# Transposes by VectorE instead of TensorE, transfers in other steps, and later phases in source order, in a fused state-space and two-layer feed-forward kernel

## The chip, the cores and the metric

The kernel runs on one core of one Trainium2 chip. The time is the device time of one execution in microseconds; several executions are measured and the median is told. A profile of one more execution gives the trace, whose times are counted from its first instruction. Engines are called by the profile's names: PE (TensorE), PEld (its weight loads), ACT (ScalarE), DVE (VectorE), POOL (GpSimd), SP (SyncE, which issues all DMAs here).

## The reference

Three stages, one behind the other, all in float32 at the interface:

```python
# 1. state-space attention: batch 4, 8 heads, 768 positions, head size 32, state size 16
cum = cumsum(log(clip(a)))                        # within a chunk
y   = ((C @ B.T) * exp(cum_i - cum_j) * causal) @ x  +  (C @ state) * exp(cum_i)
state = exp(sum) * state + sum_j B_j x_j exp(cum_last - cum_j)
# 2. x: (3072, 256), the heads side by side
h = max(x @ w1, x @ w2, x @ w3)                   # (3072, 768)
y = h @ w_out                                     # (3072, 256)
# 3.
h = y @ w_in                                      # (3072, 2048)
out = (max(h, 0) + alpha * min(h, 0)) @ w_out2    # (3072, 256)
```

The weights come as float64. The result is the same for any chunk length in stage 1.

## The kernel before

**Feed-forward layers.** Every operand is kept as two halves, a rounded one and the rest, and a product is three matmuls (`parts`, L582). Tokens go in six tiles of 512. Layer 1 has six units per tile (128 of 768 inner features): `up1` does three times six matmuls, ACT and DVE take the maximum, `halves` splits the result on ACT (`gh`) and POOL (`gl`). Layer 2 has sixteen units per tile: `up2` does six matmuls, two DVE instructions, then `halves`. `down` does six matmuls for a unit and comes two units after its `up` (`LAG`). The order of tiles is in `PHASES`: (1,0), (1,1), (2,0), (1,2), (2,1), (1,3), (2,2), (1,4), (2,3), (1,5), (2,4), (2,5), layer first; the fourth phase is (1,2). The two last `down`s of a phase are carried into the next one's first two units. They end with `end1` (L644), which splits a layer-1 tile into `yt`, or with `end2` (L652), which copies the transposed result out of PSUM (ACT one half, DVE the other), transposes it back with eight PE transposes in two batches (L664), copies each batch out and stores it. Both phases' accumulators are the same two PSUM banks.

**Attention.** 24 blocks of 128 positions of one sequence with all heads. Blocks 0 to 11 (two sequences) are direct: chunks of 64, nothing passes through DRAM. Blocks 12 to 23 are wide (`r >= NDIR`): one chunk of 128. For a wide block `att_t` (L337) transposes B, C and the decayed C (`cp`, none in the first block of a sequence) on PE (L344), copies them out and splits B and C in halves on ACT and DVE (L347 to L355), and stores the halves in a DRAM tile `sc` (L357). `att_l` loads them back in eight DMAs in a layout in which four heads stack on the partitions (L374, L376). `att_b` multiplies C with B (L419) and with the decay (L421). `att_e` makes the decay: eight exponentials on ACT (L402), two masks on POOL (L403). `att_a` multiplies B and C by their decays on POOL (L335), `att_y` makes the result (L487, L490) and its halves `xt` (L520, L521), `att_u` the state, and asks for the next rows of the cumulative sums (L321).

**Order.** The first blocks, up to L737, are written out in order by hand, in a manual schedule. Behind that a planner orders each engine's instructions by itself, from priorities and estimated times; the source gives it the work in this order: between the units, `attend` takes the next steps of a list (`rounds`, L524), so many that the blocks are done a little ahead of the tile that needs them (`quota`), and `slot` takes steps of the weights' conversion. A round has five steps. PE, ACT, DVE, POOL and SP each execute their instructions in the order that came out.

Of the kernel before, what the change touches and what calls it, by code (L numbers as in the profile page):

```python
# [9 lines left out]
F32 = mybir.dt.float32  # L10
# [9 lines left out]
P = 128  # L20
# [17 lines left out]

LEADW = 12288
START = 4  # L40
LAG = 2
# [33 lines left out]
def fused(ctx: ExitStack, tc: tile.TileContext, x, a, B, C, w1, w2, w3, w_out, v_in, v_out, alpha, cst, out):  # L75
# [133 lines left out]
    def load(r):  # L209
        if r < NR:  # L210
            load_bc(r)
            load_x(r)

    def load_bc(r):
        b, k = divmod(r, NB)
# [6 lines left out]
    def load_x(r):  # L222
        b, k = divmod(r, NB)
        d = blk[r]
# [11 lines left out]
    s_cum = yy.tile([P, 2, 512], F32R, tag="yt0", name="yt0").rearrange("p a b -> p (a b)")[:BT * H, :S].bitcast(F32)  # L236
    s_la = const.tile([P, NB, BT * H], F32, name="la")
    first = const.tile([P, Q], F32, name="first")
    never = const.tile([P, Q], BF16, name="never")
    one_b = const.tile([P, P], BF16, name="one_b")  # L240
    warm = un.tile([P, 512], F32, tag="g", name="g")[:, :256].bitcast(BF16)
# [86 lines left out]
    def att_a(r, only=None):  # L328
        b, k = divmod(r, NB)
        d = blk[r]  # L330
        for key, src, w, used in (("bp", "b", dec_b, r < NDIR or k < NB - 1), ("cp", "c", dec_c, r < NDIR or k)):
# [3 lines left out]
            nc.gpsimd.tensor_tensor(o, d[src], w[:, k, b, :].unsqueeze(2).to_broadcast([P, H, N]), ALU.mult)  # L335

    def att_t(r, part=None):  # L337
        d = blk[r]
        keys = [("b", "c"), ("cp",), ("b", "c", "cp")][2 if part is None else part]
        if r >= NDIR and r % NB == 0:  # L340
            keys = ("b", "c")
        pt = ptile(ps_at, "at", (P, 3, P)) if part is None else ptile(ps_acc, "acc", (P, 3, P))
        for i, key in enumerate(keys):
            nc.tensor.transpose(pt[:, i, :], d[key].rearrange("p h n -> p (h n)"), ident)  # L344
        if "cp" in keys:
            cpt = d["cpt"] = sm.tile([P, P], F32, tag="cpt", name="cpt")
            nc.scalar.activation(cpt, pt[:, len(keys) - 1, :], AF.Copy)  # L347
        if r >= NDIR:
            ts = sm.tile([P, 6, P], F32R, tag="ts", name="ts", bufs=1)
            nc.scalar.activation(ts[:, 0, :], pt[:, 0, :], AF.Copy)  # L350
            for i in range(2):
                nc.scalar.activation(ts[:, 2 + i, :], pt[:, 1, :], AF.Copy, scale=par[i])
            nc.vector.tensor_tensor(ts[:, 1, :], pt[:, 0, :], ts[:, 0, :], ALU.subtract)
            for i in range(2):
                nc.vector.scalar_tensor_tensor(ts[:, 4 + i, :], pt[:, 1, :], par[i], ts[:, 2 + i, :], ALU.mult, ALU.subtract)  # L355
            sc = d["sc"] = dr.tile([P, 6, P], F32, tag="sc", name="sc")
            nc.sync.dma_start(sc, ts.bitcast(F32))  # L357
        elif "b" in keys:
            bs = d["bs"] = stk.tile([P, 2, P], F32, tag="bs", name="bs")
            cs = d["cs"] = stk.tile([P, 2, P], F32, tag="cs", name="cs")  # L360
            for i in range(2):
# [3 lines left out]
    def att_l(r):  # L365
        if r < NDIR:
            return
        d = blk[r]
        sc = d["sc"]
        bs = d["bs"] = v_tile().bitcast(F32R).rearrange("p (v t) -> p v t", v=4)  # L370
        cs = d["cs"] = st_tile().bitcast(F32R).rearrange("p (v e t) -> p v e t", v=4, e=2)
        for c in range(4):
            o = slice(32 * c, 32 * c + 32)
            nc.sync.dma_start(bs[o].bitcast(F32), sc[:, c // 2, :].rearrange("(v q) t -> q v t", v=4))  # L374
            h = 2 + 2 * (c % 2)
            nc.sync.dma_start(  # L376
                cs[o].bitcast(F32).rearrange("q v e t -> q v (e t)"),
                sc[:, h:h + 2, :].rearrange("(v q) e t -> q v (e t)", v=4),
            )
# [32 lines left out]
    def att_b(r):  # L412
        d = blk[r]
        if r >= NDIR:
            for g in range(2):
                cb = ptile(ps_at, "at")
                for v in range(2):
                    m = d["cs"][:, 2 * g + v, :, :].rearrange("p e t -> p (e t)")
                    nc.tensor.matmul(cb[:, v * 256:(v + 1) * 256], d["bs"][:, 2 * g + v, :], m, start=True, stop=True)  # L419
# [231 lines left out]

    def end2(ph, lo=0, n=512):  # L652
        t = ph[1]
# [85 lines left out]
    if True:  # L739
# [12 lines left out]
        owed, at = 0.0, 0  # L752
        for ph in PHASES:
            layer, t, _, pace = ph
            up, end = (up1, end1) if layer == 1 else (up2, end2)
            pend = []
            for f, o, n, _, blocks, _ in units_of(ph):
                until(blocks)
                owing[1] = pace or quota_w(at)
                pend.append((f, o, n, up(ph, f, o, n)))  # L760
                if carry:
                    carry.pop(0)()
                elif tail:
                    tail.pop(0)()
                if len(pend) > LAG:
                    down(ph, *pend.pop(0))
                slot()
                if layer == 2:
                    slot()
                owed += quota(at)  # L770
                at += 1
                while owed > 0.999 and todo:
                    owed -= 1
                    attend()
            for i, u in enumerate(pend):
                def go(ph=ph, u=u, finish=end if i == LAG - 1 else None):
                    down(ph, *u)
                    if finish:
                        finish(ph)
                carry.append(go)  # L780
        for go in tail:
            go()
        tail.clear()
        for u in pend[:-1]:
            down(ph, *u)
        f, _, _, g = pend[-1]
        for o, n in LAST:
            down(ph, f, o, n, [x[:, o:o + n] for x in g])
            end2(ph, o, n)
            while tail:  # L790
                tail.pop(0)()

# [24 lines left out]
```

## Time and profile before

| | |
|---|---|
| median of 3 runs | 560.87 us (560.72 to 562.03) |
| the profiled execution | 561.31 us, span 559.60 us |
| PE busy | 545.7 us (98%), clock granted 0.997 |
| PEld, DVE, ACT, POOL busy | 441.4, 325.7, 233.0, 223.4 us |
| DMA | 48.52 MB, 118943 packets |

The span is the time from the first to the last instruction of the trace; the execution's own time is a little longer. A busy PE is counted by modelled ends of its matmuls, so what bounds it is read from the chain of waits and from single stretches.

### The profile page before, as it was taken

Reading aid. Unit: us, or ns where it says so; the run is one execution under the profiler, and the core shown is the slowest. Engines: PE = TensorE matmul, PEld = TensorE weight load, DVE = VectorE, ACT = ScalarE, POOL = GpSimd, SP = SyncE. Lnnn points to the kernel's source line nnn. Section 1 sums busy time; section 2 is a strip of 40 time slices with the busy share of each in tenths; the row PEclk is TensorE's granted clock in tenths of the full one; section 3 lists DMA queues with packets and bytes.
Section 4 is the critical chain, followed back from the end, with each engine's and each line's share of the span. In section 5 each row is a group of like instructions: output and inputs, shape, how many; then the busy total and the mean of one; then the engine's idle time right before and its main releaser. Section 6 shows DMA issues by size and latency. Waiting matters only on the chain.

```text
span 559.6 us, 9832 instructions
## 1 busy us (share of the span) xinstructions
PE 545.7 (98%) x3615; PEld 441.4 (79%) x3616; DVE 325.7 (58%) x600; ACT 233.0 (42%) x588; POOL 223.4 (40%) x232
## 2 busy tenths in 40 slices
PE   8889999989999999999999999999999999999997
PEld 4767878767778888888788888888877888888885
DVE  5886898986654446664346665446664235555553
ACT  5666687953333344343334343443322312222222
POOL 2143445534543234454234544323543214444441
PEclk9998999999999999999999999999999999999999
DMA  8877888730222443514444433333110000000001
GB/s 146 224 145 175 187 178 237 204 78 10 40 59 66 125 99 97 138 43 104 109 108 105 110 70 103 87 107 109 49 38 1 20 19 1 0 2 19 20 0 38
DMA packets 118943, 48.52 MB, mean 87 GB/s; under 512 B 80752, under 2 KB 108848, under 8 KB 118896
## 3 DMA queue, kind: packets, MB, share of 16 engines
q1 hardware_dynamic: 118896, 47.90, 34.8%
q8 instruction: 28, 0.46, 0.4%
q14 instruction: 19, 0.16, 0.1%
HBM read 39.82 MB, written 8.06 MB: 86 GB/s over the span
## 4 chain that ended last, share of the span: by engine, by line
PE 85%; DVE 6%; ACT 3%; issue 2%; DMA 2%; SPq 1%; POOL 0%; DVEq 0%; POOLq 0%; ACTq 0%
PE up L587 46%; PE acc L587 31%; DVE v L168 2%; PE at L490 1%; PE up L664 1%; PE at L344 1%; PE at L419 1%; DMA st<-in_moe_w_dram 1%; SPq L232 1%; DVE g L611 1%; DMA e<-cum_w 1%; PE at L487 1%; PE up L682 1%; DVE v L166 1%; PE at L503 1%
## 5 line engine op out<-in xcount | busy, mean ns | idle before, releaser
L127 POOL TENSOR_TENSOR gl<-g,gh 128x512 fp32r<-128x512 f32 (+1 forms) x137 | 172.1, 1256 | 259.9 <-ACT gh L126 246.4
L126 ACT ACTIVATE gh<-g 128x512 fp32r<-128x512 f32 (+1 forms) x138 | 84.5, 612 | 235.9 <-DVE g L622 156.2
L587 PE MATMUL up<-xt,w 128*128 128x512 f32 (+1 forms) x756 | 164.0, 366 | 2.6 <-DVE g L611 1.1
L587 PEld LDWEIGHTS up<-xt,w 128*128 128x128 f32 x756 | 128.6, 190 | 27.7 <-issue 2.9
L587 PE MATMUL up<-yt,vi 128*128 128x512 f32 x576 | 148.9, 394 | 0.0
L587 PEld LDWEIGHTS up<-yt,vi 128*128 128x128 f32 x576 | 106.3, 188 | 23.0 <-issue 0.9
L621 DVE TENSOR_SCALAR g<-up,alph 128x512 f32<-128x512 f32 x96 | 72.0, 750 | 89.1 <-PE up L587 80.3
L587 PE MATMUL acc<-gh,vo 128*128 128x512 f32 (+1 forms) x392 | 120.0, 387 | 0.2 <-DVE yt L650 0.2
L611 DVE TENSOR_TENSOR g<-up,g 128x512 f32<-128x512 f32 (+1 forms) x84 | 51.5, 613 | 71.7 <-PE up L587 71.0
L587 PEld LDWEIGHTS acc<-gh,vo 128*128 128x128 f32 x392 | 73.0, 188 | 15.3 <-DVE yt L650 0.6
L587 PE MATMUL acc<-gl,vo 128*128 128x512 f32 (+1 forms) x196 | 75.8, 387 | 0.0
L622 DVE SCALAR_TENSOR_TENSOR g<-up,g 128x512 f32<-128x512 f32 x96 | 66.4, 691 | 3.2
L587 PE MATMUL acc<-gh,wo 128*128 128x512 f32 (+1 forms) x168 | 47.4, 366 | 0.2 <-ACT gh L126 0.2
L587 PEld LDWEIGHTS acc<-gl,vo 128*128 128x128 f32 x196 | 36.8, 188 | 7.7 <-DVE gl L127 0.2
L402 ACT ACTIVATE e<-e,ncum 128x128 f32<-128x128 f32 x96 | 31.0, 390 | 8.1 <-DMA e<-cum_w 8.1
L587 PEld LDWEIGHTS acc<-gh,wo 128*128 128x128 f32 x168 | 29.6, 189 | 4.9 <-ACT gh L126 0.4
L609 ACT ACTIVATE g<-up 128x512 f32<-128x512 f32 (+1 forms) x42 | 22.5, 535 | 24.0 <-PE up L587 21.0
L587 PE MATMUL acc<-gl,wo 128*128 128x512 f32 (+1 forms) x84 | 30.3, 361 | 0.0
L521 DVE TENSOR_TENSOR xt<-at,xt 128x128 fp32r<-128x128 f32 x48 | 12.9, 287 | 19.2 <-ACT xt L520 19.2
L168 DVE SCALAR_TENSOR_TENSOR v<-st,v 128x512 uint32<-128x512 uint32 x28 | 22.7, 813 | 1.2 <-ACT st L159 0.8
L407 ACT ACTIVATE e<-e,ncum 128x64 f32<-128x64 f32 x80 | 21.7, 345 | 2.8 <-DMA e<-cum_d 2.8
L410 POOL TENSOR_SCALAR_AFFINE_SELECT e<-e 64x512 f32<-64x512 f32 x20 | 15.8, 792 | 13.0 <-ACT e L407 12.3
(120 smaller groups left out, 422.7 us busy)
## 6 DMA issues: line engine op xcount, KB each, us to landing
e<-cum_w SPq DMA_DIRECT2D x24, 256.0 KB, 4.1
st<-sc SPq DMA_DIRECT2D x48, 128.0 KB, 2.6
st<-in_moe_w_out_dram SPq DMA_DIRECT2D x11, 512.0 KB, 5.0
st<-in_moe_w_dram SPq DMA_DIRECT2D x9, 512.0 KB, 5.2
sc<-ts SPq DMA_DIRECT2D x12, 384.0 KB, 2.3
st<-in_moe_w_in_dram SPq DMA_DIRECT2D x8, 512.0 KB, 4.6
v<-sc SPq DMA_DIRECT2D x48, 64.0 KB, 2.4
out_dram<-st SPq DMA_DIRECT2D x11, 256.0 KB, 2.2
```

Of the source, the lines that this page charges most:

```text
L126: nc.scalar.activation(dst_h, src, AF.Copy)
L127: engine.tensor_tensor(dst_l, src, dst_h, ALU.subtract)
L168: nc.vector.scalar_tensor_tensor(v, hi, 3, v, ALU.logical_shift_left, ALU.bitwise_or)
L402: nc.scalar.activation(e[:, q, :], e[:, q, :], AF.Exp, bias=ncum[:, k, b, 4 * g + q:4 * g + q + 1])
L407: nc.scalar.activation(e[:, h, :], e[:, h, :], AF.Exp, bias=ncum[:, k, b, h:h + 1])
L410: nc.gpsimd.affine_select(out=m, in_=m, pattern=[[0, H], [1, Q]], compare_op=ALU.is_ge, fill=0.0, base=0, channel_multiplier=-1)
L521: nc.vector.tensor_tensor(xt[t][1][:, g, o], yp[g], xt[t][0][:, g, o], ALU.subtract)
L587: nc.tensor.matmul(acc, w, r, start=(first and i == 0), stop=(last and i == len(todo_) - 1), skip_group_check=True)
L609: nc.scalar.activation(g, p, AF.Copy)
L611: nc.vector.tensor_tensor(g, p, g, ALU.max)
L621: nc.vector.tensor_scalar(g, p, 0.0, alph[:, f:f + 1], ALU.min, ALU.mult)
L622: nc.vector.scalar_tensor_tensor(g, p, 0.0, g, ALU.max, ALU.add)
```

## The change

The result (`end2`): two DVE transposes of 32x32 blocks straight out of PSUM, and four DMAs that put the blocks in their places; the last tile keeps the old way as `end2_last`, in a manual schedule. Wide blocks: B and C are split before the transpose, by ACT and POOL, into a tile `tok` of 768 columns whose zeros keep the two heads of a pair apart (`att_s`); DVE transposes the 32x32 blocks of `tok` and of the decayed C (`att_t`), four DMAs store them with the blocks in place, and `att_l` loads them, the decayed C too. The three stand in three different steps of a round, the loads of B and C come a block earlier. For direct blocks `att_t` joins the step of `att_b`, and `load` has a step of its own. From the fourth phase on, each phase is a manual schedule: every engine's instructions in the order of the source, with `attend` ahead of `carry` and `down`, and in layer 2 the second carried `down` ahead of the second unit. Some constants move into the buffer that later holds the transposed halves, and B's and C's masked transposes of direct blocks share one tile.

```diff
+STRICT = 3
+AHEAD = 10
     def load(r):
-        if r < NR:
-            load_bc(r)
-            load_x(r)
+        for q in (r, r + 1)[r > AHEAD:1 + (r >= AHEAD)]:
+            load_bc(q)
+        load_x(r)
...
+    def att_s(r):
+        if r < NDIR:
+            return
+        d = blk[r]
+        if not tok:
+            tok.append(stk.tile([P, 6, P], F32R, tag="bc", name="tok"))
+            nc.vector.memset(tok[0].bitcast(F32), 0.0)
+        t = tok[0]
+        def heads(s):
+            flat = t.rearrange("p s c -> p (s c)")[:, (s + 2) * P - 2 * (P + N):(s + 2) * P].rearrange("p (e c) -> p e c", e=2)
+            return flat[:, :, N:].rearrange("p e (v c) -> p e v c", v=4)[:, :, :, N:]
+        bh, c = d["b"].rearrange("p h n -> p (h n)"), d["c"].rearrange("p (v e) n -> p e v n", e=2)
+        nc.scalar.activation(t[:, 0, :], bh, AF.Copy)
+        nc.scalar.activation(heads(2), c, AF.Copy)
+        nc.gpsimd.tensor_tensor(t[:, 1, :], bh, t[:, 0, :], ALU.subtract)
+        nc.gpsimd.tensor_tensor(heads(4), c, heads(2), ALU.subtract)
     def att_t(r, part=None):
         d = blk[r]
+        if r >= NDIR:
+            ts = sm.tile([P, 7 * P], F32, tag="ts", name="ts", bufs=1)
+            used = 6 + (r % NB > 0)
+            nc.vector.transpose(ts[:, :6 * P], tok[0].bitcast(F32).rearrange("p s c -> p (s c)"))
+            if used > 6:
+                nc.vector.transpose(ts[:, 6 * P:], d["cp"].rearrange("p h n -> p (h n)"))
+            sc = d["sc"] = dr.tile([7, P, P], F32, tag="sc", name="sc")
+            for i in range(4):
+                o = slice(32 * i, 32 * i + 32)
+                nc.sync.dma_start(sc[:used, :, o].rearrange("s (v q) t -> q (s v) t", v=4), ts[o, :used * P].rearrange("q (w t) -> q w t", t=32))
+            return
...
-        if r >= NDIR:
-            ts = sm.tile([P, 6, P], F32R, tag="ts", name="ts", bufs=1)
...
-            nc.sync.dma_start(sc, ts.bitcast(F32))
     def att_l(r):
...
+        if r % NB:
+            cpt = d["cpt"] = sm.tile([P, P], F32, tag="cpt", name="cpt")
+            nc.sync.dma_start(cpt, sc[6])
...
     def rounds(r0):
         for r in range(r0, NR):
-            def first(r=r):
-                if r + 1 < NR:
-                    att_l(r + 1)
-                if r + 2 < NR:
-                    att_a(r + 2)
-            yield first, 0
+            if r + 2 < NR:
+                yield lambda r=r: att_a(r + 2), 0
             yield lambda r=r: (att_y(r), r + 1 < NR and att_u(r + 1)), r + 1
-            if r + 1 < NR:
+            if r + 2 < NR:
+                late = r + 2 == NDIR
+                yield lambda r=r, late=late: (att_e(r + 1), late or att_s(r + 2)), 0
+                yield lambda r=r, late=late: (att_b(r + 1), att_s(r + 2) if late else att_t(r + 2)), 0
+                yield lambda r=r, late=late: (late and att_t(r + 2), load(r + 3), att_l(r + 2)), 0
+            elif r + 1 < NR:
                 yield lambda r=r: att_e(r + 1), 0
                 yield lambda r=r: att_b(r + 1), 0
-            if r + 2 < NR:
-                yield lambda r=r: (att_t(r + 2), load(r + 3)), 0
...
+    def end2(ph):
+        t = ph[1]
+        z = st_tile().bitcast(F32).rearrange("p (c t) -> p c t", c=2)
+        for c in range(2):
+            nc.vector.transpose(z[:, c, :], acc[2, t][c])
+        dst = out[512 * t:512 * (t + 1), :].rearrange("(t b) (c a) -> b c t a", b=32, c=2)
+        for i in range(4):
+            o = slice(32 * i, 32 * i + 32)
+            nc.sync.dma_start(dst[:, :, :, o], z[o].rearrange("b c (t a) -> b c t a", a=32))
...
-        for ph in PHASES:
+        for n_ph, ph in enumerate(PHASES):
+            with tc.manual_schedule() if n_ph >= STRICT else nullcontext():
...
+                    if n_ph >= STRICT and layer == 2 and len(pend) == 1:
+                        carry.pop(0)()
+                    pend.append((f, o, n, up(ph, f, o, n)))
+                    owed += quota(at)
+                    at += 1
+                    while n_ph >= STRICT and owed > 0.999 and todo:
+                        owed -= 1
+                        attend()
+                    if carry:
+                        carry.pop(0)()
+                    elif tail:
+                        tail.pop(0)()
+                    if len(pend) > LAG:
+                        down(ph, *pend.pop(0))
```

## Rows read from the trace of the kernel before

**Rows 1.** Busy time by stretch: us, then each engine's busy us (x instructions)

```profile
core 0: us, PE busy (x) PEld busy (x) DVE busy (x) ACT busy (x) POOL busy (x), PEclk, DMA share, GB/s
82.00:124.00 42.00, 40.49 (x325) 32.42 (x326) 37.23 (x69) 32.25 (x85) 19.81 (x23) 1.00 0.66 170
124.00:172.00 48.00, 47.80 (x337) 37.90 (x337) 28.79 (x53) 14.75 (x35) 22.43 (x23) 1.00 0.24 53
172.00:209.00 37.00, 37.00 (x194) 30.23 (x192) 15.57 (x30) 14.54 (x37) 11.20 (x13) 1.00 0.35 86
```

**Rows 2.** Chain of waits, pieces between 186 and 301: start us, us, what

```profile
203.33 0.33 PE at L344 x3
203.66 4.12 PE up L587 x18
...
281.17 0.44 PE up L664 x4
281.61 1.39 PE acc L587 x6
...
288.96 0.22 PE at L344 x2
...
293.31 1.36 PE acc L587 x6
```

**Rows 3.** Groups of one shape: line, engine, operation, count | busy us, mean ns

```profile
L664 PE MATMUL up<-ct,v 128*128 128x128 f32 x48 | 8.1, 277 | 0.9 <-ACT v L655 0.7
...
L355 DVE SCALAR_TENSOR_TENSOR ts<-at,ct,ts 128x128 fp32r<-128x128 f32 x24 | 7.2, 342 | 0.0
...
L353 DVE TENSOR_TENSOR ts<-at,ts 128x128 fp32r<-128x128 f32 x12 | 3.5, 292 | 14.8 <-ACT ts L352 14.8
...
L656 DVE COPY v<-acc 128x512 f32<-128x512 f32 x5 | 3.4, 690 | 2.7 <-PE acc L587 2.7
```

**Rows 4.** Timeline from 508 to 513, one unit of layer 2: start us, us

```profile
508.24 1.52 PE L587 MATMUL up<-yt,vi 128*128 128x512 f32 x6
...
509.87 0.75 DVE L621 TENSOR_SCALAR g<-up,alph 128x512 f32<-128x512 f32 x1 [1.24 <-PE up L587]
...
510.65 0.69 DVE L622 SCALAR_TENSOR_TENSOR g<-up,g 128x512 f32<-128x512 f32 x1
...
511.44 0.63 ACT L126 ACTIVATE gh<-g 128x512 fp32r<-128x512 f32 x1 [0.37 <-DVE g L622]
...
512.15 1.28 POOL L127 TENSOR_TENSOR gl<-g,gh 128x512 fp32r<-128x512 f32 x1 [1.41 <-ACT gh L126]
```

**Rows 5.** Timeline from 299 to 307, ACT, DVE and POOL beside a unit

```profile
299.72 0.41 POOL L335 TENSOR_TENSOR bp<-b,dec_b 128x128 f32<-128x128 f32 x1
...
300.75 1.28 ACT L649 ACTIVATE yt<-acc 128x512 fp32r<-128x512 f32 x2 [2.07 <-PE acc L587]
...
301.54 1.28 DVE L650 TENSOR_TENSOR yt<-acc,yt 128x512 fp32r<-128x512 f32 x2
...
304.98 2.14 ACT L402 ACTIVATE e<-e,ncum 128x128 f32<-128x128 f32 x7
...
306.39 0.64 POOL L403 TENSOR_SCALAR_AFFINE_SELECT e<-e 128x512 f32<-128x512 f32 x1
```

**Rows 6.** Timeline from 118 to 134, the end of phase (1,1); idle before in brackets

```profile
127.74 0.40 ACT L402 ACTIVATE e<-e,ncum 128x128 f32<-128x128 f32 x1 [4.05 <-DMA e<-cum_w]
...
130.80 0.73 PE L587 MATMUL acc<-gh,vo 128*128 128x512 f32 x2 [0.20 <-DVE yt L650]
```

**Rows 7.** DMA issues: count, KB each, median us from issue to landing

```profile
st<-sc SPq DMA_DIRECT2D x48, 128.0 KB, 2.6
...
sc<-ts SPq DMA_DIRECT2D x12, 384.0 KB, 2.3
...
c<-in_C_dram SPq DMA_DIRECT2D x24, 64.0 KB, 3.0
...
cum_d<-yt SPq DMA_DIRECT2D x2, 48.0 KB, 4.0
```

**Rows 8.** Timeline of SP from 312 to 317: start us, us of one issue

```profile
315.53 0.42 SPq L376 DMA_DIRECT2D st<-sc  x1
```

More of the change, by code (lines that the diff above doesn't have):

```diff
@@ L1 @@
-from contextlib import ExitStack
+from contextlib import ExitStack, nullcontext
 import numpy as np
@@ L222, in load_x @@
     def load_x(r):
+        if r >= NR:
+            return
         b, k = divmod(r, NB)
-        d = blk[r]
+        d = blk.setdefault(r, {})
         d["x"] = xm[r % NX]
@@ L236, in fused @@
     s_cum = yy.tile([P, 2, 512], F32R, tag="yt0", name="yt0").rearrange("p a b -> p (a b)")[:BT * H, :S].bitcast(F32)
[L237 to L240, printed above, removed]
+    scr = sm.tile([P, 7 * P], F32, tag="ts", name="scr", bufs=1)
+    s_la = scr[:, :NB * BT * H].rearrange("p (k h) -> p k h", k=NB)
+    first = scr[:, 192:192 + Q]
+    never = scr[:, 256:256 + Q // 2].bitcast(BF16)
+    one_b = scr[:, 288:288 + P // 2].bitcast(BF16)
     warm = un.tile([P, 512], F32, tag="g", name="g")[:, :256].bitcast(BF16)
@@ L335, in att_a @@
             nc.gpsimd.tensor_tensor(o, d[src], w[:, k, b, :].unsqueeze(2).to_broadcast([P, H, N]), ALU.mult)
+    tok = []
+    def att_s(r):
+        if r < NDIR:
+            return
+        d = blk[r]
[11 more added lines that the diff above has]
+        nc.gpsimd.tensor_tensor(heads(4), c, heads(2), ALU.subtract)
     def att_t(r, part=None):
         d = blk[r]
+        if r >= NDIR:
[8 more added lines that the diff above has]
+                nc.sync.dma_start(sc[:used, :, o].rearrange("s (v q) t -> q (s v) t", v=4), ts[o, :used * P].rearrange("q (w t) -> q w t", t=32))
+            return
         keys = [("b", "c"), ("cp",), ("b", "c", "cp")][2 if part is None else part]
-        if r >= NDIR and r % NB == 0:
-            keys = ("b", "c")
         pt = ptile(ps_at, "at", (P, 3, P)) if part is None else ptile(ps_acc, "acc", (P, 3, P))
@@ L347, in att_t @@
             nc.scalar.activation(cpt, pt[:, len(keys) - 1, :], AF.Copy)
-        if r >= NDIR:
-            ts = sm.tile([P, 6, P], F32R, tag="ts", name="ts", bufs=1)
[L350 to L356, printed above, removed]
-            nc.sync.dma_start(sc, ts.bitcast(F32))
-        elif "b" in keys:
-            bs = d["bs"] = stk.tile([P, 2, P], F32, tag="bs", name="bs")
-            cs = d["cs"] = stk.tile([P, 2, P], F32, tag="cs", name="cs")
+        if "b" in keys:
+            bc = stk.tile([P, 6, P], F32R, tag="bc", name="bc").bitcast(F32)
+            bs, cs = d["bs"], d["cs"] = bc[:, :2], bc[:, 2:4]
             for i in range(2):
@@ L369, in att_l @@
         sc = d["sc"]
+        if r % NB:
+            cpt = d["cpt"] = sm.tile([P, P], F32, tag="cpt", name="cpt")
+            nc.sync.dma_start(cpt, sc[6])
         bs = d["bs"] = v_tile().bitcast(F32R).rearrange("p (v t) -> p v t", v=4)
[L371 removed]
+        cs = d["cs"] = st_tile().bitcast(F32R).rearrange("p (e v t) -> p e v t", v=4, e=2)
         for c in range(4):
             o = slice(32 * c, 32 * c + 32)
[L374 removed]
+            nc.sync.dma_start(bs[o].bitcast(F32), sc[c // 2].rearrange("(v q) t -> q v t", v=4))
             h = 2 + 2 * (c % 2)
             nc.sync.dma_start(
[L377 to L378 removed]
+                cs[o].bitcast(F32).rearrange("q e v t -> q (e v) t"),
+                sc[h:h + 2].rearrange("e (v q) t -> q (e v) t", v=4),
             )
@@ L650, in end1, with end2_last @@
             nc.vector.tensor_tensor(yt[t][1][:, c, :], p, yt[t][0][:, c, :], ALU.subtract)
-    def end2(ph, lo=0, n=512):
+    def end2(ph):
[7 more added lines that the diff above has]
+            nc.sync.dma_start(dst[:, :, :, o], z[o].rearrange("b c (t a) -> b c t a", a=32))
+    def end2_last(ph, lo, n):
         t = ph[1]
@@ L752, in fused @@
         owed, at = 0.0, 0
-        for ph in PHASES:
[L754 to L763, printed above, removed]
-                    tail.pop(0)()
[L765 to L791, printed above, removed]
+        for n_ph, ph in enumerate(PHASES):
+            with tc.manual_schedule() if n_ph >= STRICT else nullcontext():
+                layer, t, _, pace = ph
+                up, end = (up1, end1) if layer == 1 else (up2, end2)
+                pend = []
+                for f, o, n, _, blocks, _ in units_of(ph):
+                    until(blocks)
+                    owing[1] = pace or quota_w(at)
+                    if n_ph >= STRICT and layer == 2 and len(pend) == 1:
[12 more added lines that the diff above has]
+                        down(ph, *pend.pop(0))
+                    slot()
+                    if layer == 2:
+                        slot()
+                    while owed > 0.999 and todo:
+                        owed -= 1
+                        attend()
+                for i, u in enumerate(pend):
+                    def go(ph=ph, u=u, finish=end if i == LAG - 1 else None):
+                        down(ph, *u)
+                        if finish:
+                            finish(ph)
+                    carry.append(go)
@@ L794 @@
+        with tc.manual_schedule():
+            for u in pend[:-1]:
+                down(ph, *u)
+            f, _, _, g = pend[-1]
+            for o, n in LAST:
+                down(ph, f, o, n, [x[:, o:o + n] for x in g])
+                end2_last(ph, o, n)
+                while tail:
+                    tail.pop(0)()
 _INS = ['x', 'a', 'B', 'C', 'moe_w1', 'moe_w2', 'moe_w3', 'moe_w_out', 'moe2_w_in', 'moe2_w_out', 'moe2_alpha']
```

3 lines of the change are left out of this document (2 added, 1 removed).

## The prediction

> **What bounds the kernel now.** I read the page's slices first, then the busy time by stretch, then the chain of waits, then the groups of one shape. The slices show PE at 9 tenths nearly everywhere and its clock granted in full. The stretches [rows 1] say where that is a bound: from 172 us on PE is busy for the whole of a stretch (37.00 of 37.00 from 172 to 209 us), while VectorE has 15.57 of 37.00, ScalarE 14.54, GpSimd 11.20. From 124 to 172 us it is 47.80 of 48.00. Only before 124 us do other engines carry the chain: between 82 and 124 us VectorE has 37.23 of 42.00 us, with the conversion of the weights. The chain agrees: from 131 to 550 us it runs along PE, six feed-forward matmuls in 1.36 us, one piece behind another [rows 2]. So after 124 us a matmul removed moves the end by its own slot, and a wait put into PE's queue moves it back by its length. Everything that the change touches in its wide blocks and in the result's transposes lies after 124 us.
>
> **PE work removed.** (1) The result's transposes. `end2` used eight PE transposes for a 512-token tile, in two batches of four. A batch takes 0.44 us of the chain and the piece behind it 1.39 instead of 1.36 us [rows 2], so 0.47 us. The program has 48 such transposes [rows 3]; eight belong to the last tile, which keeps the old way, so ten batches go: 10 x 0.47 = 4.7 us. (2) The wide blocks' transposes of B, C and the decayed C. Three take 0.33 us and the eighteen matmuls behind them 4.12 us instead of 3 x 1.36 = 4.08: 0.37 us. A first block of a sequence has two, 0.22 us, and with the same 0.04 behind it 0.26 us [rows 2]. There are twelve wide blocks (twelve stores of the halves, rows 7), ten of which have a state to multiply, all but the first of either sequence: 10 x 0.37 + 2 x 0.26 = 4.2 us. Together 8.9 us, all of it from stretches in which PE has no idle time. Nothing is added to PE.
>
> **What VectorE, ScalarE and GpSimd get.** No transpose on VectorE is in the trace, so I bound it. A 128-column instruction takes 0.29 us and a 512-column one 0.69 us [rows 3]: 0.29 + 0.40 x (columns - 128) / 384. That gives 0.96 us for the 768 columns of the halves, 0.29 for the decayed C, 0.69 for each half of the result. Below, a transpose might be as short as a 128-column instruction whatever its width (0.29); above, I allow twice the slope's value, since blocks have to be gathered and written out (1.9 us for the 768 columns). I take the slope's value, because all the VectorE rows of this size lie near it. VectorE then changes per wide block by 0.96 + 0.29 - 0.29 - 2 x 0.34 = +0.3 us, and ScalarE loses the copies. For the result, VectorE has two instructions where it had a copy of 0.69 and a copy out of about the same, and ScalarE loses two. GpSimd gets two subtractions of 128 columns per wide block, 0.41 us each if they cost as much as its product of that size [rows 5]. VectorE is less than two thirds busy after 124 us, so as sums these cost nothing; if that cover were gone, 12 x 0.3 = 4 us would be their whole size.
>
> **Source order from the fourth phase on.** Here lies the price that I expect. In order, a unit's result must pass VectorE, VectorE, ScalarE, GpSimd: after the up matmuls end at 509.76, the instructions start at 509.87, 510.65, 511.44 and 512.15, the last for 1.28 us [rows 4]. So `gl` is there 3.7 us after the up matmuls. `down` of a unit comes two units later: down, up, down, up at 1.36 us each, and its third matmul, the first that reads `gl`, 0.45 us later: 5.9 us. The slack is 2.2 us. What the planner interleaved by itself now stands in whole steps: eight exponentials run on end (seven in 2.14 us, so eight in 2.45) behind a unit's `gh` and ahead of the next one's, followed now by two copies of about 0.25 us, while GpSimd does two masks of 0.64 us and the two subtractions [rows 5].
>
> I walked the quotas through the code to see which step falls into which unit. In an ordinary place of layer 2, with a unit's up matmuls ending at 0: `gh` 1.7 to 2.3, exponentials to 4.8, copies to 5.2, masks and subtractions to 6.4, the next `gl` 6.4 to 7.7; it is wanted at 2.7 + 5.9 = 8.6. No stall, 0.9 us left. The next unit has the product with CB and the transposes: VectorE comes free at 8.3, the `gl` after it ends at 11.7 and is wanted at 11.8. Nothing is left there, but nothing is lost.
>
> In the phases (2,1) and (2,2) the step with the exponentials falls into the second unit, right behind the end of the layer-1 tile, whose four instructions on the accumulator hold ScalarE and VectorE (1.28 us each, the second starting 0.79 us after the first, rows 5). That puts everything 0.8 us later: `gl` of the unit after is there 0.8 us too late and, with the transposes in front of the next, that one 1.1 us: 1.9 us a place, 3.8 us in two. The other end is nothing, for which the trace has a case: at 127.74 ScalarE had waited 4.05 us at just such a phase boundary, and PE stood still for 0.20 us behind it [rows 6]. I take the middle, 1 us a place, 2.0 us in all, because that case is the nearest row and my figures leave several tenths open on each step.
>
> Layer-1 units last 5.4 us, so steps that fall in pairs into one of them (two places) find their slack. The end of the kernel keeps its order: PE's ten transposes and matmuls between two chunks already stood interleaved, and what follows waits for copies either way: 0, with 0.3 us to either side.
>
> **Stores and loads.** A wide block's halves go out one step earlier relative to their loads, in four DMAs of 128-byte pieces, 3584 in all (7 x 128 rows of 4), instead of one DMA in 3 KB pieces that landed in 2.3 us [rows 7]. Nothing in the trace stores such pieces. A load of 1024 pieces of 64 bytes lands in 3.0 us; at that rate for all of them (3.0 x 3.5) the store takes 10.5 us, and 2.3 us if the pieces cost nothing. I take 6. SP's queue waits for the landing before it issues the nine loads of that block; behind it stand the next block's rows of e, wanted five steps later, and at phase starts the result's stores, which nobody waits for. The loads are wanted by `att_b` at the next round. From one store to that is seven units of layer 2 (19 us) or, twice, three units of layer 1 (16 us). Transposes 1.3, store 6, nine issues at 0.42 us [rows 8] 4, landing 2.6 [rows 7]: 14 us. That is hidden, with 2 us left in the two short places.
> The Trainium skill, in "DMA: Bandwidth & Descriptors", section "Specifications", says that a transfer needs at least 512 bytes for line rate and that below it the engine reads, modifies and writes. The trace neither confirms nor denies it: the one store of short pieces, the cumulative sums in 256-byte pieces, landed in 4.0 us for 48 KB [rows 7], which is slower than the 2.3 us of 384 KB in long pieces, and faster than the rule alone would lead one to fear. By the rule the store would be near its long end, and its rival below the likelier.
>
> **Before 124 us.** The direct blocks keep their instructions; their transposes stand one step earlier, B and C's tile is one instead of two, constants share the buffer of the halves and are read before it is needed. Any of these moves shifts the planner's order. I put 0, with 1.5 us to either side.
>
> **Sum.** The profiled execution took 561.31 us (span 559.60). 561.31 - 8.9 + 2.0 = 554.4. The median of the runs is 560.87, 0.44 lower; so 554.0 for the median.
>
> **Rivals.** (a) No stall in source order: everything removed from PE shows: 560.87 - 8.9 = 552.0, 550.5 with a lucky start. For it: the 0.20 us at 130.80 [rows 6], and engines with idle time around each unit. Against it: the 0.1 us left at the ordinary product step. (b) Slower: the two steps with exponentials and transposes stall PE in every wide round. The mechanism is the queue of VectorE in order: the transposes wait for GpSimd's subtractions and the next unit's maximum stands behind them. It decides at 8.9 / 12 = 0.74 us per wide block. If a transpose takes twice the slope's value, the 768 columns are 1 us longer, of which 0.1 us has cover: 0.9 us a block, in the four ordinary places of layer 2 and more in the boundary ones; were all twelve blocks hit by that and the 1 us more by late `gl`, 12 x 1.0 + 2.0 = 14 us against 8.9: 566. With half of it 559.5. (c) The stores in short pieces: landing in 10.5 us instead of 6 uses up the 2 us and leaves 2.5 us in each of the two layer-1 places, 5 us: 559.0. The page's rule speaks for it. (d) The halves arrive as before but the planner's order of the first three phases gets worse by 2 to 3 us: 556.5.
>
> **Chances.** The forecast (554.0, its own range 552.8 to 557) 0.45; (a) 0.27; (d) 0.07; (c) 0.09; (b) 0.12. This measurement can tell 0.3%, 1.7 us, from no change: 559.2 and 562.5 are the bounds. Faster: forecast, (a), (d) and half of (c) make 0.84. Within: the other half of (c) and the mild end of (b), 0.07. Slower: the rest of (b), 0.09. The range goes from 550.5, the good end of (a), to 559.5, the mild end of (b) and (c).
>
> **What will show it.** Right: no PE transposes from line `end2` but those of the last tile, none of wide blocks; six matmuls still 1.36 us; stretches from 172 us on shorter by 0.47 us a batch and 0.37 us a block; idle PE time, or late pieces, only in the second to fourth units of (2,1) and (2,2), released by GpSimd's `gl`. Wrong: PE idle in most wide rounds, released by `gl` and behind it VectorE's transposes; or PE's `att_b` matmuls waiting for a DMA into `cs` or `bs`; or the time up to 124 us moved by more than 2 us.

## The result, and the profile after

The changed kernel took 554.46 us (median of 4 runs, 553.52 to 555.93), the kernel before 561.04 beside it: a ratio of 0.988, 95% interval 0.986 to 0.990. Two later sessions, on two chips, gave 557.38 (ratio 0.992, 0.990 to 0.995) and 556.27 (0.990, 0.987 to 0.993); the median over all sixteen runs is 556.5. The profiled execution took 553.52 us, the fastest of the four, its span 551.8.

The busy times and the packets, from the page of the changed kernel:

```profile
PE 536.2 (97%) x3541; PEld 432.4 (78%) x3542; DVE 330.5 (60%) x587; ACT 221.6 (40%) x556; POOL 235.0 (43%) x256
...
DMA packets 185632, 49.84 MB, mean 90 GB/s; under 512 B 144112, under 2 KB 177072, under 8 KB 185584
```

PE has lost 9.5 us, against 545.7 before; ScalarE has lost 11, VectorE has gained 5 and GpSimd 12, and there are 66,700 more packets. The stretches that answer to [rows 1], and three more with a wait in them (columns as there):

```profile
82.00:124.00 42.00, 40.64 (x315) 31.86 (x314) 36.75 (x69) 30.84 (x77) 22.27 (x22) 1.00 0.67 171
124.00:172.00 48.00, 47.37 (x336) 37.68 (x335) 29.29 (x49) 14.52 (x33) 22.47 (x22) 1.00 0.27 50
172.00:209.00 37.00, 37.00 (x215) 30.17 (x214) 17.48 (x31) 10.80 (x27) 12.57 (x15) 1.00 0.57 106
209.00:252.00 43.00, 42.58 (x245) 34.24 (x244) 29.13 (x48) 15.82 (x40) 23.21 (x25) 1.00 0.53 108
...
295.00:340.00 45.00, 44.58 (x247) 35.99 (x246) 29.83 (x48) 16.56 (x44) 24.05 (x27) 1.00 0.47 98
...
382.00:425.00 43.00, 42.57 (x229) 34.17 (x228) 24.72 (x40) 15.22 (x39) 22.02 (x21) 1.00 0.30 64
```

PE is still the bound, and 0.42 to 0.43 us of it is idle in each of three stretches; the 0.63 us from 124 to 172 us lie ahead of the source order, nearly all in one wait behind the end of phase (1,1). The groups that answer to [rows 3], with the columns of that view:

```profile
L373 DVE STREAM_TRANSPOSE ts<-tok 128x768 f32<-128x768 f32 x12 | 11.7, 975 | 1.5 <-POOL tok L366 1.5
...
L689 DVE STREAM_TRANSPOSE st<-acc 128x512 f32<-128x512 f32 x10 | 7.0, 716 | 0.5 <-PE acc L619 0.5
...
L366 POOL TENSOR_TENSOR tok<-c,tok 128x128 fp32r<-128x128 f32 x12 | 5.6, 464 | 0.0
...
L375 DVE STREAM_TRANSPOSE ts<-cp 128x128 f32<-128x128 f32 x10 | 2.7, 270 | 0.0
...
L707 PE MATMUL up<-ct,v 128*128 128x128 f32 x8 | 2.1, 314 | 0.5 <-ACT v L698 0.2
```

Of the 48 PE transposes of the result, the eight of the last tile are left, and none of the wide blocks'. The first wait behind 132 us is at 223.40; the timeline ahead of it (start, us, instruction, in brackets the idle time of the engine before it) shows what is new:

```profile
218.20 0.47 POOL L366 TENSOR_TENSOR tok<-c,tok 128x128 fp32r<-128x128 f32 x1
...
218.70 0.98 DVE L373 STREAM_TRANSPOSE ts<-tok 128x768 f32<-128x768 f32 x1 [0.16 <-POOL tok L366]
219.60 0.27 DVE L375 STREAM_TRANSPOSE ts<-cp 128x128 f32<-128x128 f32 x1
...
219.79 0.71 DVE L653 TENSOR_SCALAR g<-up,alph 128x512 f32<-128x512 f32 x1
...
220.54 0.69 DVE L654 SCALAR_TENSOR_TENSOR g<-up,g 128x512 f32<-128x512 f32 x1
...
221.34 0.63 ACT L129 ACTIVATE gh<-g 128x512 fp32r<-128x512 f32 x1 [3.31 <-DVE g L654]
...
222.05 2.68 POOL L130 TENSOR_TENSOR gl<-g,gh 128x512 fp32r<-128x512 f32 x2 [2.14 <-ACT gh L129]
...
223.40 0.50 PE L619 MATMUL acc<-gl,vo 128*128 128x512 f32 x1 [0.42 <-POOL gl L130]
```

It goes by VectorE's queue. GpSimd's subtraction into `tok` lets the transposes start, and behind them stand the two instructions (219.79, 220.54) of a unit whose up matmuls had ended at 217.0. `gh` waits for these and `gl` for `gh`: GpSimd stood idle for 2.14 us before that `gl`, which ends at 223.35, and PE, which wants it, had 0.42 us idle. The same stands at 307.37. A third wait, at 390.09, is of another kind: `PE at L452` waits 0.43 us for the load of a block's halves.

### The profile page after: what moved, and what is told of

It is laid out like the page before. It is cut to its first block, busy times and chain, and to the rows that moved or that the text cites. A ratio compares the mean times of both kernels' runs of the same rounds, so it can differ in the third digit from the quotient of the medians.

```text
span 551.8 us, 9739 instructions
## 1 busy us (share of the span) xinstructions
PE 536.2 (97%) x3541; PEld 432.4 (78%) x3542; DVE 330.5 (60%) x587; ACT 221.6 (40%) x556; POOL 235.0 (43%) x256
## 4 chain that ended last, share of the span: by engine, by line
PE 77%; DVE 7%; ACT 4%; DMA 4%; issue 3%; SPq 2%; POOL 1%; ACTq 0%; DVEq 0%; POOLq 0%
PE up L619 41%; PE acc L619 29%; DVE v L171 2%; PE at L523 1%; ACT e L440 1%; DMA st<-in_moe_w_out_dram 1%; DVE g L643 1%; PE at L452 1%; POOL gl L130 1%; DMA st<-in_moe_w_in_dram 1%; DMA e<-cum_w 1%; DMA e<-cum_d 1%; DVE e L467 1%; PE at L520 1%; ACT st L162 1%
## 5 line engine op out<-in xcount | busy, mean ns | idle before, releaser
L619 PE MATMUL up<-xt,w 128*128 128x512 f32 (+1 forms) x756 | 161.5, 363 | 2.5 <-ACT g L641 1.7
L619 PE MATMUL up<-yt,vi 128*128 128x512 f32 x576 | 146.0, 390 | 0.0
L619 PEld LDWEIGHTS up<-yt,vi 128*128 128x128 f32 x576 | 107.7, 188 | 23.0 <-issue 0.4
L435 ACT ACTIVATE e<-e,ncum 128x128 f32<-128x128 f32 x96 | 29.6, 388 | 4.5 <-DMA e<-cum_w 4.5
L443 POOL TENSOR_SCALAR_AFFINE_SELECT e<-e 64x512 f32<-64x512 f32 x20 | 17.1, 856 | 14.9 <-ACT e L440 14.1
L454 DVE TENSOR_TENSOR e<-at,e 128x512 f32<-128x512 f32 x24 | 16.0, 686 | 10.4 <-POOL e L436 10.4
```

What stands on the lines that cost most here:

```text
L435: nc.scalar.activation(e[:, q, :], e[:, q, :], AF.Exp, bias=ncum[:, k, b, 4 * g + q:4 * g + q + 1])
L443: nc.gpsimd.affine_select(out=m, in_=m, pattern=[[0, H], [1, Q]], compare_op=ALU.is_ge, fill=0.0, base=0, channel_multiplier=-1)
L454: nc.vector.tensor_tensor(ef, cb, ef, ALU.mult)
L619: nc.tensor.matmul(acc, w, r, start=(first and i == 0), stop=(last and i == len(todo_) - 1), skip_group_check=True)
```

## The experiments

Each kernel's times were taken beside runs of the kernel before on the same chip; ratios are to those.

**1. The planner's order kept.**

```diff
-STRICT = 3
+STRICT = 99
```

> The change without its source order: all phases up to the last tile's end are left to the planner. My theory (source order costs about 2 us of stalls at phase starts and gives nothing): PE full as before, 8.9 us of transposes gone, 561.0 - 8.9 + 0 = 552, some 2 us under the changed kernel, and no waits of PE for gl from 172 us on. Rival (source order is needed for the gain, since the planner places the new steps badly): 556 or more, with idle PE in the wide rounds.

574.47 us, ratio 1.024 (1.021 to 1.027): slower than the kernel before. The rival was right. PE's waits in this kernel (us in all, times, the longest) and two stretches:

```profile
PE up L619 <- ACT xt L553: 2.1, 1, 2.1
PE at L452 <- DMA v<-sc: 2.0, 1, 2.0
PE at L520 <- DVE e L454: 1.8, 4, 1.2
```

```profile
340.00:382.00 42.00, 37.28 (x225) 28.71 (x224) 18.18 (x36) 15.99 (x45) 14.02 (x20) 0.92 0.71 143
...
425.00:462.00 37.00, 34.06 (x181) 26.60 (x180) 15.38 (x26) 10.12 (x23) 10.22 (x9) 0.95 0.26 50
```

Steps that the planner now orders by itself come late for the layer-1 tile that needs their block: the longest wait is for its `xt`. PE is idle for 4.7 us around the start of (1,4) and 2.9 us around that of (1,5), and the granted clock there is below full. From 124 to 540 us PE's waits come to 9.4 us, against 1.8 in the changed kernel. The 7.6 us between are less than half of the 18.6 us by which the two differ in the table under 10; the rest, the lower clock among it, was not told apart.

**2. The result's transposes alone**, in the kernel before: the new `end2` for five tiles, planner's order.

```diff
-    def end2(ph, lo=0, n=512):
+    def end2(ph):
+        ...
+        for c in range(2):
+            nc.vector.transpose(z[:, c, :], acc[2, t][c])
+    def end2_last(ph, lo, n):
```

> The kernel before with only the result's transposes on VectorE for five tiles. My theory (PE slots are the price, ten batches of 0.47 us): 561.0 - 4.7 = 556.3, 0.8% faster. Rival (two VectorE instructions end to end hold the accumulator longer than a copy on either engine, and the next tile's down waits): gain under 3 us, PE idle at phase starts.

563.46 us, ratio 1.004 (1.002 to 1.006): the gain of 4.7 us is gone, and yet, against the rival, PE waits for nothing behind 131 us in its trace (of an execution of 560.37, the fastest of twelve). Counted in start-to-start times of PE's matmuls from 135 to 550 us, the pairs with a transpose of the result fall by 5.8 us (2.3 of it the slots of ten feed-forward matmuls, which stay), and the attention's small matmuls are cut into more runs between the feed-forward ones: `att_y` follows a feed-forward matmul 18 times instead of 14 and is followed by one 13 times instead of 3, `att_u` follows one 6 times instead of never. All pairs with a matmul of the attention together take 6.2 us more than in the kernel before. That the planner cut them up because of the changed queue was not tried by itself.

**3. Wide blocks and source order, without the result's transposes.**

```diff
-                up, end = (up1, end1) if layer == 1 else (up2, end2)
+                up, end = (up1, end1) if layer == 1 else (up2, lambda ph: end2_last(ph, 0, 512))
```

> The changed kernel with the result's transposes back on PE for all tiles, all else as changed. My theory: the changed kernel's 554.5 + 4.7 = 559.2. Rival (source order hides these transposes, or they cost more when nothing is interleaved): 556 or 562.

566.42 us, ratio 1.008 (1.005 to 1.010): leaving out the one part costs 9 to 12 us against the three medians of the changed kernel, not 4.7, more than either expectation had. PE's largest wait, the timeline (start, us, instruction, in brackets the idle time before it) and the stretches there:

```profile
PE up L619 <- DVE st L713: 4.0, 2, 2.1
```

```profile
199.71 0.98 DVE L373 STREAM_TRANSPOSE ts<-tok 128x768 f32<-128x768 f32 x1 [0.15 <-POOL tok L366]
200.61 0.27 DVE L375 STREAM_TRANSPOSE ts<-cp 128x128 f32<-128x128 f32 x1
200.80 0.65 DVE L713 COPY st<-up 128x512 f32<-128x512 f32 x1
...
201.51 1.94 PE L619 MATMUL up<-xt,w 128*128 128x512 f32 x5 [2.10 <-DVE st L713]
```

```profile
199.00:201.50 2.50, 0.41 (x2) 0.00 (x0) 2.35 (x5) 0.01 (x1) 0.68 (x2) 1.00 0.00 0
201.50:203.50 2.00, 1.99 (x6) 1.61 (x7) 0.55 (x1) 0.00 (x0) 0.00 (x0) 0.67 0.75 116
203.50:205.50 2.00, 2.00 (x6) 1.51 (x6) 0.69 (x1) 0.63 (x1) 0.09 (x1) 0.50 0.89 147
```

With PE's transposes back, PE needs the PSUM buffer that a VectorE copy empties, and that copy now stands behind the blocks' transposes: 2.10 us idle. Then the clock column falls to 0.50, which is 1.2 GHz, and the next twelve matmuls take 4.61 us of the chain instead of 2.72. So a wait of 2.1 us costs 4.0. The other, of 1.9 us at 290 us, is followed by 4.61 us for twelve matmuls too and costs 3.8. With the 4.7 us of slots that makes 12.5; the table under 10 has 11.9 to 12.8 us between this kernel and the changed one.

**4. Source order alone**, in the kernel before.

```diff
+            with tc.manual_schedule() if n_ph >= STRICT else nullcontext():
...
```

Source order means two things here as in the changed kernel: the order is fixed, and `attend` comes ahead of `carry` and `down`. They were not tried one by one.

> The kernel before with its phases from the fourth on in source order and nothing else changed. My theory (source order takes 1 us at each of two phase starts and gives nothing): 561.0 + 2 = 563, up to 565 since its transposes of a wide block make PE wait for products of GpSimd. Rival (the order of the steps, not their being strict, was the limit before): 561 or less.

563.36 us, ratio 1.003 (1.001 to 1.005). As expected. PE waits for the result's copy, at 202 and at 289 us, the waits of experiment 3 without the transposes in front:

```profile
PE up L588 <- DVE st L671: 1.3, 2, 0.7
```

**5. Source order and the result's transposes, wide blocks as before** (experiments 2 and 4 together).

> The kernel before with two of the three parts: source order from the fourth phase on, and the result transposed by VectorE for five of the six tiles; the wide blocks keep their old path (TensorE transposes, halves in one step). It closes a two-by-two with three kernels already measured in source order: neither transpose part 563.4, wide blocks alone 566.4, both 554.5 to 557.4. Theory A (the prediction's sum: each removed slot is worth its slot, and nothing else): 563.4 - 4.7 = 558.7. Theory B (the result's transposes through TensorE sit behind a VectorE copy, and in source order TensorE waits for that copy at the layer-2 ends, 1.04 and 1.06 us in the kernel with source order alone, 2.49 and 2.29 us in the one with the wide blocks on VectorE; the new result path takes away slots and both waits): 563.4 - 4.7 - 2.1 = 556.6 or a little less, and then no PE wait for a VectorE copy of the result is in the trace. The two are told apart by those two waits more than by the 2 us of time.

557.59 us, ratio 0.993 (0.990 to 0.995). No wait for a VectorE copy is left, as theory B has it; in their place stand two shorter ones, for DMAs:

```profile
PE at L420 <- DMA st<-sc: 0.4, 1, 0.4
PE at L420 <- DMA out_dram<-st: 0.3, 1, 0.3
```

In source order the four combinations are 563.4 (neither), 557.6 (result), 566.4 (wide blocks), and 554.5 to 557.4 (both): the wide blocks' part costs 3 us without the result's, and brings 1.3 us with it, taken on one chip (557.59 and 556.27). The 1.3 us are within the noise (0.990 to 0.995 against 0.987 to 0.993). The traces say the same more clearly: by the table under 10 that part costs 4.1 us without the result's and brings 1.9 to 2.8 with it.

**6. The 768-column transpose done twice.**

```diff
-            nc.vector.transpose(ts[:, :6 * P], tok[0].bitcast(F32).rearrange("p s c -> p (s c)"))
+            for _ in range(2):
+                nc.vector.transpose(ts[:, :6 * P], tok[0].bitcast(F32).rearrange("p s c -> p (s c)"))
```

> The changed kernel with the 768-column transpose of each wide block done twice, the second a repetition into the same place: 0.98 us more of VectorE per wide block, 11.7 us in all. By the working of the prediction (0.1 us of cover in an ordinary layer-2 place): about 0.9 us in each of four ordinary places and 1.0 in each of two at phase starts, 559 to 560 us. Rival (there is a unit's time of cover, since the measured waits were a third of those worked out): 555.5 or less, waits only near 222 and 306 us, longer by up to 1 us each.

558.30 us, ratio 0.994 (0.992 to 0.997); the changed kernel on the same chip took 557.38, so 12 us more of VectorE's time cost 0.9 us by the medians, which is within the noise (0.992 to 0.997 against 0.990 to 0.995), and 2.3 us by the two traces (table under 10). PE's waits:

```profile
PE acc L620 <- POOL gl L130: 1.2, 2, 0.6
PE acc L620 <- ACT gh L129: 1.0, 2, 0.5
```

They stand at 227 and 228 and at 312 and 314 us, in the two places that already had one: there PE is now idle for 1.1 us a place instead of 0.4, so the transposes are on the path. The ordinary places, for which the prediction counted 0.1 us of cover, still have none; an added 0.98 us was covered there. The time fits neither expectation, the places are the rival's.

**7. No step in the second unit of a source-order layer-2 phase.**

```diff
-                    while n_ph >= STRICT and owed > 0.999 and todo:
-                        owed -= 1
-                        attend()
+                    if n_ph >= STRICT and layer == 2:
+                        if f != 1 and owed > 0.999 and todo:
+                            owed -= 1
+                            attend()
+                    else:
+                        ...
...
-                    while owed > 0.999 and todo:
+                    while (n_ph < STRICT or layer == 1) and owed > 0.999 and todo:
```

> The changed kernel with no attention step in the second unit of a layer-2 phase in source order, and one step a unit at most, so that the exponentials no longer stand right behind the end of a layer-1 tile. My theory (that step makes gl late there): PE's two waits of 0.6 us near 222 and 306 us go, the one near 389 us stays, the time falls by about 1.2 us to 553.3. Rival (gl is late because of the transposes alone, wherever the step stands): the two waits move one unit on, and the time stays.

> The parent of the held step again (no step in the second unit of a source-order layer-2 phase), on the same chip as the changed kernel and the held step, to compare the three: 1 to 2.5 us below the changed kernel if the two waits at the low parts of the block's product, 0.6 us each, are all that it removes or if it also keeps the clock up; the same within 0.5 us if the step it displaces only moves the waits.

555.10 us in the second session (ratio 0.989, 0.986 to 0.992) and 555.87 in the third (0.989, 0.987 to 0.992), 2.3 and 0.4 us below the changed kernel beside it. Both `gl` waits are gone:

```profile
209.00:252.00 43.00, 43.00 (x248) 35.08 (x247) 29.96 (x48) 15.82 (x40) 23.21 (x25) 1.00 0.54 110
```

A wait of 0.6 to 0.8 us for a DMA has come at 318 us, and the one at 390 us is still there (1.0 and 1.2 us). So little time is won where the step was moved: from the 433rd to the 2160th feed-forward matmul (table under 10) the two traces are 0.8 and 0.1 us shorter than those of the changed kernel beside them. The 1.2 us of the first expectation did not come; the 2.3 us of the second session lie mostly ahead of the moved steps, where its trace is 2.9 us shorter.

**8. Besides, no step in the last unit of any layer-1 phase.**

```diff
+                        while n_ph >= STRICT and owed > 0.999 and todo and f < NF1 - 1:
...
```

> As the variant without a step in the second unit of layer 2, and with no step in the last unit of a layer-1 phase either, so that block 22's loads are issued ahead of the next rows of e. My theory: all three waits of PE between 200 and 400 us go, 554.5 - 1.8 = 552.7. Rival (steps pushed together elsewhere make new waits): 554 or more, with waits of PE in other places.

559.88 us, ratio 0.996 (0.994 to 0.998): the theory was wrong, the rival right. The wait at 390 us is gone, but held back in every phase the steps come late elsewhere, at 240 and at 325 us, and the longer one is again followed by a lower clock (0.96 from 295 to 340 us):

```profile
PE at L452 <- DMA e<-cum_w: 2.4, 1, 2.4
PE at L452 <- DMA st<-sc: 1.5, 1, 1.5
```

**9. That step held back in phase (1,4) alone**, on top of experiment 7.

```diff
+                        while n_ph >= STRICT and owed > 0.999 and todo and (n_ph, f) != (7, NF1 - 1):
...
```

> The kernel with no step in the second unit of a source-order layer-2 phase, and besides no step in the last unit of the one phase (1,4), so that the loads of the third wide block of the second batch row are issued before and not behind the load of the decay rows that waits for a buffer. Theory: the wait of 0.6 us that the changed kernel has at 389 us (1.2 us in this kernel's parent) goes and nothing comes in its place: 0.6 to 1.2 us below the parent. Rival: the held step comes later, in the next phase, and the product step behind it is then late, as when the last unit was skipped in every phase, where waits of 1.9 and 2.8 us appeared: 1 to 3 us above the parent.

553.97 us, ratio 0.987 (0.984 to 0.990): 1.9 us below its parent (555.87) and 2.3 below the changed kernel (556.27) on the same chip, the lowest median of all. The intervals overlap with both, but the trace is clear: from the 433rd matmul on it is 2.8 us shorter than its parent's. The block whose loads are moved is block 22, the fifth wide one of its sequence and not the third. SP's timeline, of the changed kernel first, then of this one (start, us, instruction):

```profile
369.14 2.42 SPq L379 DMA_DIRECT2D sc<-ts  x4
...
381.05 1.15 SPq L329 DMA_DIRECT2D e<-cum_w  x2
382.38 0.37 SPq L402 DMA_DIRECT2D cpt<-sc  x1
...
386.17 0.43 SPq L409 DMA_DIRECT2D st<-sc  x1
```

```profile
370.85 2.43 SPq L379 DMA_DIRECT2D sc<-ts  x4
...
375.59 0.34 SPq L402 DMA_DIRECT2D cpt<-sc  x1
...
379.53 0.43 SPq L409 DMA_DIRECT2D st<-sc  x1
385.46 0.93 SPq L329 DMA_DIRECT2D e<-cum_w  x2
```

In the changed kernel the loads stand behind the rows of `e`, whose buffer PE frees at 381 us (the queue waits 8.6 us for it); here they stand ahead of them. PE's only wait from 124 to 540 us is one that ends at 132.5 us, so the parent's wait at 319 us has gone too, and the gain is more than the theory's 0.6 to 1.2:

```profile
PE acc L619 <- DVE yt L682: 0.6, 1, 0.6
```

**10. The changed kernel again.**

> The changed kernel once more, beside the variants of this call: 554.5 us within 1.5.

> The changed kernel a third time, on the chip of the other three: 554 to 557.5, the spread of its ten timed runs so far. If the difference between its two sessions (554.5 and 557.4) is the granted clock before 124 us, then its profile shows a clock under 0.97 in 82 to 124 us where its time is over 556, and 0.99 or more there where it is under 555.

557.38 us in the second session, 1.4 us outside the first expectation, and 556.27 in the third. To compare sessions I count PE's feed-forward matmuls, 2172 in each kernel, and take the starts of the 433rd (early in phase (2,0)) and of the 2160th:

```
kernel                           433rd at   2160th at   between
before                             126.4      552.2      425.8
changed, first session             124.6      544.1      419.5
changed, second session            128.3      548.2      419.9
changed, third session             128.2      548.6      420.4
planner's order (1)                126.3      564.4      438.1
result on PE (3)                   125.5      557.8      432.3
source order alone (4)             126.8      555.0      428.2
source order + result (5)          126.2      548.5      422.3
transpose twice (6), second        128.6      550.8      422.2
second unit free (7), second       125.4      544.5      419.1
second unit free (7), third        125.3      545.6      420.3
held step (9)                      127.7      545.2      417.5
```

Behind the 433rd the three traces of the changed kernel agree within 0.9 us; ahead of it they are 3.7 apart. Idle time and clock differ there. The second session, then the first, from 112 to 120 us:

```profile
112.00:116.00 4.00, 2.60 (x12) 1.80 (x10) 4.00 (x7) 2.54 (x7) 1.47 (x2) 1.00 0.99 222
116.00:120.00 4.00, 3.11 (x8) 2.47 (x9) 3.90 (x9) 3.37 (x9) 1.02 (x1) 0.68 0.01 1
```

```profile
112.00:116.00 4.00, 2.76 (x13) 1.93 (x12) 4.00 (x8) 3.57 (x11) 2.13 (x1) 1.00 0.64 123
116.00:120.00 4.00, 3.88 (x18) 2.88 (x17) 3.40 (x6) 2.01 (x4) 2.30 (x2) 1.00 0.00 0
```

PE waits here behind the weights' conversion on VectorE in both. In one session it was idle for 2.3 us of the eight and the clock fell; in the other for 1.4 and it stayed. The expectation named 82 to 124 us as the place of the fall; in the third session it was elsewhere, at 76 to 82 us (0.96 from 47 to 82 us, and 0.99 behind), so that part of it missed.

## Why the prediction was right, and where it was not

The forecast of 554.0 us stands against 554.46, inside its range. By its steps:

**PE work removed, 8.9 us.** Right in size. With no wait left in the source order (experiment 9), the stretch behind the 433rd matmul is 425.8 - 417.5 = 8.3 us shorter. The changed kernel has 5.4 to 6.3 of it.

**VectorE's and GpSimd's instructions.** The slope gave 0.96, 0.29 and 0.69 us; measured are 0.975, 0.270 and 0.716. GpSimd's subtraction takes 0.46 instead of 0.41, which was one row; the group of that product had a mean of 0.47 in the trace of before.

**Stalls of source order, 2.0 us.** Half right. The waits lie in (2,1) and (2,2), behind `gl`, as worked out from [rows 4 to 6], and experiment 7 shows that the step in the second unit makes them. But the prediction had two late `gl`s a place, by 0.8 and 1.1 us, and only the one behind the transposes is late: from the start of the matmul before to the start of the one that waited it is 0.81 us instead of 0.23, so 0.6 a place and 1.2 in two. Some 0.6 us more came from a wait that the prediction had excluded, and had put among its signs of being wrong (`att_b` waiting for a DMA into `cs`): it let the rows of `e` stand behind the loads in SP's queue, while in one place, the last unit of (1,4), they stand ahead. Experiment 9 shows this one. The 2.0 us were the middle between 0 and 3.8; that the sum of 1.8 came so near was luck, since the reason was partly another. The 0.1 us of cover in the ordinary places was too small: 0.98 us more of VectorE's time found cover there (experiment 6).

**"Here lies the price".** This was the step that read the change the wrong way round. The prediction priced source order against a planner that would go on as before. Experiments 1, 2, 4 and 5 show otherwise: the planner's order with the new work costs 18 to 20 us more than source order (ratios 1.024 against 0.988 to 0.992), though in the kernel before source order is 2.3 us slower. The parts don't add, in source order either: by the table under 10 the result's part brings 5.9 us there without the wide blocks' and 11.9 to 12.8 with them, because waits for a VectorE copy, and the lower clock behind the longer ones, go together with the 4.7 us of slots. A sum over slots holds only where no wait comes or goes with them.

**Stores of short pieces, 6 us.** Near. The four DMAs that answer to [rows 7] landed in 3.0 us each, their four issues take 2.42 us, so about 5 us by my estimate:

```profile
sc<-ts SPq DMA_DIRECT2D x40, 112.0 KB, 3.0
...
out_dram<-st SPq DMA_DIRECT2D x22, 128.0 KB, 3.3
```

The Trainium skill, in "DMA: Bandwidth & Descriptors", section "Specifications", says that for transfers below 512 bytes the engine reads, modifies and writes; the prediction set its rival (c) beside that. These pieces have 128 bytes: the four stores took about twice the 2.3 us of the one in long pieces [rows 7], and the long end of 10.5 us did not come. Whether the engine read and modified for them no trace shows.

**Before 124 us, 0 with 1.5 to either side.** Too narrow. The 433rd matmul started 1.8 us earlier than in the trace of before in the first session, and 1.9 and 1.8 us later in the other two. As far as one trace a session can tell, this is why the first session's median agrees with the forecast to 0.5 us, which is luck; 556.27 lies inside the forecast's own range of 552.8 to 557, 557.38 just outside it. Whether the changed kernel falls to the lower clock there more often than the kernel before isn't settled: only one trace of before was read.

**Rivals.** (a) is what experiment 9 approaches, at 553.97 instead of 552.0. (b) fell: even with a doubled transpose no ordinary place waits, though its mechanism, VectorE's queue in order, is what makes the two waits at the phase starts. (Half of its 14 us gives 559.0, not 559.5.) (c) fell by the stores' times. (d), 2 to 3 us lost in the first three phases, has the size of what the second and third sessions show, but they show it for the same program that gained there in the first.

A page's rule that spoke against the change was not weighed ahead: the Trainium skill, in "VectorE: DVE Perf Modes", section "Rules for kernel authors", gives a 128x128 transpose to TensorE where a result in PSUM will do, and to VectorE the 32x32 ones. The measurement decides otherwise here: with the result's transposes as VectorE's blocks, put in place by DMAs, source order took 557.59 us (experiment 5) instead of 563.36 (experiment 4). In the planner's order it brought nothing (experiment 2).

## What to carry to other kernels

Where TensorE is saturated, a removed matmul is worth its slot only if the order of the other queues stays as good; so a change of engine should be measured together with the order, and the four combinations of two parts say more than one part alone. Look at what shares a queue with the instruction that frees a buffer for the bound engine (here a unit's two instructions or a PSUM copy behind new transposes, a block's loads behind a load that waits). And count a wait of TensorE by what the clock column shows behind it, not by its length alone.

## What was not expected of the hardware

A wait of 2.10 us was followed by matmuls at 1.2 GHz, which cost another 1.9 us, while waits of 0.4 us, and one of 1.5 us in experiment 8 (at 240 us), left the clock at 1.00. And one program differed by 3.7 us ahead of 128 us between sessions, which ran on more than one chip, with the lower clock in different places, while the 420 us behind it agreed within 0.9 us.
